# Attention and feed-forward on one core: eight more attention slots early in the main loop, a scale traced one job later, and eight subtractions moved to GpSimd

## The chip, the core and the metric

The kernel runs on one core of a Trainium2 chip. The metric is the device time of one execution in microseconds (us). Five engines work in parallel, each on its own queue and in order: TensorE (PE), VectorE (DVE), ScalarE (ACT), GpSimd (POOL) and SyncE (SP), which here only issues DMAs.

## The reference

Causal attention with a decay bias feeds a two-matrix feed-forward:

```python
batch, n_heads, seq, head_dim = (8, 8, 576, 64)
scores = scale * np.matmul(q, k.transpose(0, 1, 3, 2))
cum = np.cumsum(np.maximum(s, 0.0), axis=-1)
bias = -(cum[:, :, :, None] - cum[:, :, None, :])
scores = np.where(causal, -1000000000.0, scores + np.minimum(bias, 0.0))
attn = np.exp(scores - np.max(scores, axis=-1, keepdims=True))
attn = attn / (np.sum(attn, axis=-1, keepdims=True) + 1e-09)
out = np.matmul(attn, v)
...
x = out.transpose(0, 2, 1, 3).reshape(4608, 512)
h = x @ w_in                     # 512 x 2048
g = np.where(h >= 1, h, np.where(h <= -1, 0.0, (h + 1) ** 2 / 4))
y = g @ w_out                    # 2048 x 512
```

## The kernel before, in words

**Precision.** The weights arrive as 64-bit floats and are decoded on the chip into float32 (`Weights.decode`), scaled by a bound on their size (`Weights.scale`) and split into two float16 halves, high and low (`Weights.split`). Activations are split likewise. Each feed-forward product is three float16 matmuls: high by high, low by high, high by low.

**Attention** is cut into 64 jobs: 8 batches, two halves of the sequence (`hf` 0: 320 queries, `hf` 1: 256), four pairs of heads. A job is eight *slots*, `att_slot(j, k)`: k = 0 prepares Q and K; k = 1 and 5 handle V in half 0; k = 2 to 7 are six units of scores (`s` tiles, named `s<pair>_<tile>_<head>_<column>`, numbered by pair over all batches, 0 to 31). Each unit is two matmuls (L384, L385), a minimum on DVE (L390) and an exponential on ACT (L401); `weights_t` then makes float16 halves on POOL, ACT and DVE and transposes them with a DMA from SP into `pt`. At k = 7 the *previous* job's product with V is traced (`att_out`: the tile `px<pair>_<half>`, 18 or 30 matmuls), which fills a quarter of `x` for that batch and half. The score tiles and `px` share two PSUM buffers.

**Feed-forward** is 256 steps, one for each batch, half and tile of 128 hidden columns. A step is 12 matmuls `h<batch>_<half>_<tile>` (L501), an activation on ACT and DVE (L513, L516, L517), a split on ACT and POOL (L527, L528), and two steps later 12 matmuls into `y` (L540). The last three of the 12 matmuls of an `h` read the quarter of `x` that the last `px` of that batch and half fills.

**Order.** First, four jobs of attention run beside the decoding of the first weight; its scale (`row_wi`) and split follow. Then the main loop takes 512 values of `j`: each traces one or two attention slots and half a feed-forward step. In the first 32 values a generator feeds in the second weight (`w2_tasks`: eight chunks decoded, scale, eight chunks split, twice). A scheduler then orders each engine's instructions by priority and readiness; some are given a lead (`tc.high_priority`), so the order on an engine isn't the traced one.

**What the change touches.** `batch_v(b)` reduces V to a bound; `batch_scales_v(b)` carries it across partitions with two small matmuls on PE (`row_m`, `col_m`) and gives `ex`, which the copy of `px` into `x` needs. The loop over slots:

```python
for _ in range(1 if j >= 2 * NFT else 1 + (j % 4 == 3)):
    att_slot(t // 8, t % 8)
    t += 1
```

`NFT` is 16, so 40 slots are traced in the first 32 values of `j` and one for each value after. The split of the second weight: ACT writes the high half of chunk `c` (L221); for chunks in `POOL_LO` ACT also scales the weight in place (L226) and POOL subtracts (L227), for the others DVE does both in one instruction (L229). The output of chunk `c` lies where chunk `c - 2` was held, so the high half of a chunk waits for the low half two chunks earlier.

Of the kernel before, what the change touches and what calls it, by code (L numbers as in the profile page):

```python
# [25 lines left out]
NFT = DFF // P  # L26
# [27 lines left out]
Y_LAG = 2  # L54

ACT_LOW = {'wi': range(0, 16, 2), 'wo': range(0, 16, 2)}
POOL_LO = {'wi': (2, 3, 7, 11, 15), 'wo': range(1, 16, 2)}
POOL_SCALE = ('wi',)

K_POOL = range(12)  # L60
# [13 lines left out]
def attention_ffn(ctx: ExitStack, tc: tile.TileContext, qT, kT, vT, s, w_in, w_out, yT):  # L74
# [29 lines left out]
    def column_max(src, name):  # L104

        row = ps_s.tile([P, 512], F32, tag="s", name=f"row_{name}")
        T.transpose(row[:1, :P], src, ident)
        top = ap.tile([P, 1], F32, tag="top", name=f"top_{name}")
        V.tensor_reduce(top[:1], row[:1, :P], axis=AX, op=ALU.max)
        return top[:1]  # L110

    def spread(dst, top, name):

        t16 = ap.tile([P, 1], BF16, tag="t16", name=f"t16_{name}")
        V.tensor_copy(t16[:1], top)
        col = ps_s.tile([P, 512], F32, tag="s", name=f"col_{name}")
        T.matmul(col[:, :1], ones[:1], t16[:1], start=True, stop=True)
        V.tensor_copy(dst, col[:, :1])
# [45 lines left out]
    class Weights:  # L164
        def __init__(self, name, src, held, out, tags, groups):
# [5 lines left out]
            self.raw = {}  # L171
            self.act_low, self.pool_lo = ACT_LOW[name], POOL_LO[name]

# [76 lines left out]
    def batch_v(b):  # L250
        c = csc[b] = ap.tile([P, NPAIR], F32, tag="csc", name=f"c{b}")
        r = rcs[b] = ap.tile([P, NPAIR], F32, tag="rcs", name=f"rc{b}")
        for p in range(NPAIR):
            V.tensor_reduce(c[:, p:p + 1], vraw[b, p], axis=AX, op=ALU.max, apply_absolute_value=True)
        pow2floor(c, c, TINY)
        V.reciprocal(r, c)
        V.tensor_scalar(r, r, 4096.0, None, ALU.mult)

    def batch_scales_v(b):
        t = ap.tile([P, 1], F32, tag="mt", name=f"mt{b}")  # L260
        V.tensor_reduce(t, csc[b], axis=AX, op=ALU.max)
        m = msc[b] = ap.tile([P, 1], F32, tag="mb", name=f"mb{b}")
        spread(m, column_max(t, f"m{b}"), f"m{b}")
        r = ap.tile([P, 1], F32, tag="mr", name=f"mr{b}")
        V.reciprocal(r, m)
        e = exs[b] = ap.tile([P, NPAIR], F32, tag="ex", name=f"ex{b}")
        V.tensor_scalar(e, csc[b], r, 2.0 ** -12, ALU.mult, ALU.mult)
# [51 lines left out]
    def att_prep(n, hf):  # L319

        rq, rk = raws.pop((n, hf))
        q0, N, _ = HALF[hf]
        W = q0 + N
        cd = cumd[2 * n:2 * n + 2].rearrange("h l n -> l h n")
        A.activation(Q1[:, :, :N], rq, AF.Copy, scale=-0.125)
        if jobs.index((n, hf)) < CH_N:
            for hd in range(2):
                r = ch[2 * n + hd:2 * n + hd + 1]
                CUMQ.dma_start(Q2[D:D + 2, hd, :N].bitcast(F32), r[:, :, q0:W].bitcast(F32))
                CUMQ.dma_start(K2[D + 2:D + 4, hd, :W].bitcast(F32), r[:, :, :W].bitcast(F32))  # L330
        else:
            CUMQ.dma_start(Q2[D:D + 2, :, :N].bitcast(F32), cd[:, :, q0:W])
            CUMQ.dma_start(K2[D + 2:D + 4, :, :W].bitcast(F32), cd[:, :, :W])
        A.copy(K1[:, :, :W], rk)
        A.activation(Q2[:D, :, :N], rq[:D], AF.Copy, scale=-0.125)
        V.scalar_tensor_tensor(  # L336
            Q1[D:, :, :N], rq[D:], -0.125, Q1[D:, :, :N].bitcast(F32), ALU.mult, ALU.subtract
        )
        (G if jobs.index((n, hf)) in K_POOL else V).tensor_tensor(  # L339
            K2[:D, :, :W], rk[:D], K1[:D, :, :W].bitcast(F32), ALU.subtract  # L340
        )

    def v_prep(n):

        b, p = n // NPAIR, n % NPAIR
        v = vraw.pop((b, p))
        r = rcs[b][:, p:p + 1]
        VB = ap.tile([P, 2, SP], F16, tag="vb", bufs=1, name=f"vb{n}")
        G.memset(VB[:, :, S:], 0.0)
        G.tensor_scalar(VB[:, 0, :S], v, r, 1.0, ALU.mult, ALU.mult)  # L350
        if n < V_POOL:
            G.tensor_scalar(v, v, r, 1.0, ALU.mult, ALU.mult)
            G.tensor_tensor(VB[:, 1, :S], v, VB[:, 0, :S], ALU.subtract)
        vbs[n] = VB, v, r
# [105 lines left out]

    def batch_start(b):
        batch_v(b)
        batch_scales_v(b)

    jobs = [(NPAIR * b + p, hf) for b in range(B) for hf in range(2) for p in range(NPAIR)]

    def att_slot(j, k):

        if j < len(jobs):
            n, hf = jobs[j]  # L470
            if k == 0:
                att_prep(n, hf)
            if k == 1 and hf == 0:
                v_prep(n)
            if k == V_K and hf == 0:
                v_turn(n)
            if k >= 2:
                scores(n, *UNITS[hf][k - 2])
            if k == 3 and j + 1 < len(jobs):
                att_load(*jobs[j + 1])  # L480
            if k == 1 and j % (2 * NPAIR) == V_J and j // (2 * NPAIR) + 1 < B:
                load_v(j // (2 * NPAIR) + 1)
            if k == 5 and j + 1 < len(jobs) and jobs[j + 1][0] % NPAIR == 0 and jobs[j + 1][1] == 0:
                with tc.issue_after(ttr[0]):
                    batch_start(jobs[j + 1][0] // NPAIR)
        if k == OUT_K and 1 <= j <= len(jobs) and j != NPAIR:
            while j == len(jobs) and late:
                late.pop(0)()
            att_out(*jobs[j - 1])
# [80 lines left out]
    att_load(0, 0)  # L570
    load_v(0)
    batch_start(0)
    for j in range(NPAIR):
        for k in range(8):
            if k % 2 == 0:
                c = 4 * j + k // 2
                w1.decode(c)
                w1.load(c + 3)
            att_slot(j, k)
    while late:  # L580
        late.pop(0)()
    w1.scale(0, LEAST_A)
# [22 lines left out]
    for j in range(16 * NP):  # L605
        if j % 64 == 48 and j // 64 + 1 < B:
            batch_scales(j // 64 + 1)
            batch_y(j // 64 + 1)
        for _ in range(1 if j >= 2 * NFT else 1 + (j % 4 == 3)):
            att_slot(t // 8, t % 8)  # L610
            t += 1
        with tc.high_priority(offset=W2_LEAD):
            for _ in range(W2_RATE):
                next(tasks, None)
        if j >= 2 * NFT:
            ffn_step(j // 2, j % 2)
        elif j < NFT:
            ffn_step(j, 0)
        else:
            if j == NFT:  # L620
                with tc.high_priority(offset=FFN_LEAD):
                    g_split()
            m = 2 * (j // 8 % 2)
            for i in range(j % 8 * 2, j % 8 * 2 + 2):
                ffn_y(*ffn_q[i], ms=(m, m + 1))
            if j == 2 * NFT - 1:
                del ffn_q[:NFT]
# [32 lines left out]
```

## Time and profile before

| what | value |
|---|---|
| median of three runs | 1171.36 us (1170.36 to 1180.07) |
| the profiled execution | 1178.29 us, of which the span of its instructions is 1176.2 us |
| PE busy | 1009.5 us (86% of the span) |
| DVE busy | 892.6 us (76%) |
| ACT busy | 746.0 us (63%) |
| POOL busy | 691.0 us (59%) |
| mean granted TensorE clock | 0.967 |

Busy time is a mean over stages; the stages differ, so the prediction reads the kernel in stretches of time. In rows of stretches, each engine's busy time stands beside the length, "PEclk" is the clock granted to TensorE as a share of full speed, and the DMA share is that of 16 engines. In rows of the timeline, the number in brackets is how long the engine had been idle, and what released it.

### The profile page before, as it was taken

What the parts mean: (1) busy time and instruction counts of PE and PEld (TensorE: products, weight loads), DVE (VectorE), ACT (ScalarE), POOL (GpSimd) and SP (SyncE); (2) the same over time, 40 slices, a digit from 0 to 9 for tenths busy, and PEclk for the clock granted to TensorE, in tenths of its full rate; (3) what the DMA queues carried; (4) which work ended last, traced back from release to release, by engine and by line L of the source; (5) the groups of instructions that cost most, each with busy time, mean ns of one, the idle gap of its engine ahead of it and who ended that gap; (6) DMA issues with size and microseconds to landing.
All of it is one profiled execution on the core that took longest, in us unless ns stands there. A gap on an engine that the chain in (4) does not pass through costs nothing.

```text
span 1176.2 us, 25135 instructions
## 1 busy us (share of the span) xinstructions
PE 1009.5 (86%) x8470; PEld 776.6 (66%) x8470; DVE 892.6 (76%) x2404; ACT 746.0 (63%) x1719; POOL 691.0 (59%) x1169
## 2 busy tenths in 40 slices
PE   0234678699999999799998999899989999899998
PEld 0122345487767867587767867677768867686787
DVE  6879998778777877768777777778778877787633
ACT  4656677567656765767557665667557764777533
POOL 3876268676556664656546654656557564675522
PEclk9997999799998999999999999899999999899999
DMA  8885536867637773776638672876547753767310
GB/s 243 206 195 138 165 85 145 159 139 153 130 73 180 147 148 74 166 139 144 131 84 168 152 149 65 173 142 156 119 98 172 153 133 75 163 132 157 74 34 19
DMA packets 343081, 158.04 MB, mean 134 GB/s; under 512 B 291112, under 2 KB 324264, under 8 KB 342952
## 3 DMA queue, kind: packets, MB, share of 16 engines
q1 hardware_dynamic: 333248, 146.50, 59.0%
q10 hardware_dynamic: 9704, 9.93, 2.7%
q8 instruction: 67, 1.10, 0.4%
q14 instruction: 62, 0.51, 0.1%
HBM read 75.33 MB, written 9.73 MB: 72 GB/s over the span
## 4 chain that ended last, share of the span: by engine, by line
PE 42%; DVE 8%; DMA 5%; POOL 5%; issue 3%; ACT 1%; DVEq 0%; ACTq 0%; POOLq 0%
PE y L540 18%; PE h L501 17%; DMA pt<-pb 4%; PE px L447 3%; POOL pb L422 2%; DVE pb L428 2%; PE s L384 2%; PE s L385 2%; DMA vt<-vb 2%; POOL pb L425 1%; DVE p L390 1%; DVE K L339 1%; DVE h L516 1%; DVE Q L336 1%; POOL vb L350 1%
## 5 line engine op out<-in xcount | busy, mean ns | idle before, releaser
L501 PE MATMUL h<-x,WI 128*128 128x256 f16 (+1 forms) x3072 | 453.0, 292 | 23.4 <-DVE u L517 21.0
L540 PE MATMUL y<-g,WO 128*128 128x256 f16 (+1 forms) x3072 | 453.2, 291 | 17.3 <-POOL g L528 7.4
L501 PEld LDWEIGHTS <-WI 128*128 128x128 f16 x3072 | 292.3, 100 | 118.2 <-issue 28.2
L540 PEld LDWEIGHTS <-WO 128*128 128x128 f16 x3072 | 287.1, 99 | 108.7 <-issue 19.3
L528 POOL TENSOR_TENSOR g<-u,g 128x320 f16<-128x320 f32 (+1 forms) x256 | 199.2, 778 | 209.1 <-ACT g L527 203.9
L513 ACT ACTIVATE u<-h,ub,us 128x320 f32<-128x320 f32 (+1 forms) x256 | 149.3, 584 | 171.8 <-PE h L501 146.7
L401 ACT ACTIVATE p<-p,mn 64x64 f32<-64x64 f32 (+4 forms) x320 | 178.8, 559 | 113.6 <-DVE mn L390 96.4
L516 DVE SCALAR_TENSOR_TENSOR h<-h,ws,u 128x320 f32<-128x320 f32 (+1 forms) x256 | 133.0, 520 | 118.4 <-ACT u L513 117.9
L422 POOL TENSOR_SCALAR pb<-p,rs 64x128 f16<-64x128 f32 (+4 forms) x160 | 113.7, 711 | 152.2 <-DVE rs L418 118.6
L384 PE MATMUL s<-K,Q 128*128 128x288 f32 (+4 forms) x384 | 150.9, 395 | 43.8 <-DVE mn L390 33.3
L428 DVE SCALAR_TENSOR_TENSOR pb<-p,rs,pb 64x128 f16<-64x128 f32 (+4 forms) x160 | 135.8, 849 | 52.0 <-POOL pb L422 51.6
L425 POOL TENSOR_TENSOR pb<-p,pb 64x128 f16<-64x128 f32 (+4 forms) x160 | 165.0, 1032 | 9.2
L390 DVE CUSTOM_DVE_ANT_0 p<-s,mask 64x64 f32<-64x64 f32 (+4 forms) x320 | 134.8, 422 | 41.1 <-PE s L385 36.7
L517 DVE SCALAR_TENSOR_TENSOR u<-u,r,h 128x320 f32<-128x320 f32 (+1 forms) x256 | 130.2, 510 | 7.5
L423 ACT ACTIVATE p<-p,rs 64x64 f32<-64x64 f32 (+4 forms) x160 | 89.3, 559 | 67.2 <-DVE rs L418 60.6
L385 PE MATMUL s<-K,Q 68*128 68x288 f32 (+4 forms) x384 | 121.8, 319 | 9.8 <-ACT p L423 5.5
L447 PE MATMUL px<-pt,vt 128*64 128x256 f16 (+3 forms) x1536 | 87.7, 260 | 38.0 <-DMA pt<-pb 21.8
L384 PEld LDWEIGHTS s<-K,Q 128*128 128x128 f32 (+1 forms) x384 | 74.3, 194 | 68.2 <-DVE mn L390 42.4
L527 ACT CAST g<-u 128x320 f16<-128x320 f32 (+1 forms) x256 | 108.1, 422 | 10.6 <-DVE u L517 10.6
L447 PEld LDWEIGHTS <-vt 128*64 128x64 f16 x1536 | 73.2, 113 | 61.5 <-issue 40.3
L424 POOL TENSOR_SCALAR pb<-p 64x128 f16<-64x128 f32 (+4 forms) x160 | 90.9, 569 | 6.0 <-ACT p L423 2.9
L385 PEld LDWEIGHTS s<-K,Q 68*128 68x128 f32 (+1 forms) x384 | 75.8, 198 | 12.2 <-ACT p L423 5.9
(116 smaller groups left out, 961.4 us busy)
## 6 DMA issues: line engine op xcount, KB each, us to landing
rk<-in_k_dram SPq DMA_DIRECT2D x64, 288.0 KB
rq<-in_q_dram SPq DMA_DIRECT2D x64, 160.0 KB
rk<-in_k_dram SPq DMA_DIRECT2D x64, 160.0 KB
v<-in_v_dram SPq DMA_DIRECT2D x32, 288.0 KB
wir<-in_moe_w_in_dram SPq DMA_DIRECT2D x16, 512.0 KB
rq<-in_q_dram SPq DMA_DIRECT2D x64, 128.0 KB
wor<-in_moe_w_out_dram SPq DMA_DIRECT2D x16, 512.0 KB
out_dram<-o ACTq DMA_DIRECT2D x32, 160.0 KB
```

Source lines behind the costliest of these rows:

```text
L384: T.matmul(sc[:R, :c1 - c0], Q1[:, hd, qo:qo + R], K1[:, hd, c0:c1], start=True, stop=False)
L385: T.matmul(sc[:R, :c1 - c0], Q2[:KC, hd, qo:qo + R], K2[:KC, hd, c0:c1], start=False, stop=True)
L390: ttr[0] = V.tensor_tensor_reduce(out=Pt[:R, c0:c1], in0=sc[:R, :c1 - c0], in1=mask[:R, mo:mo + c1 - c0], scale=1.0, scalar=3.0e38 if mn i ...
L401: A.activation(Pt[:R, :W], Pt[:R, :W], AF.Exp, bias=m2[:R], scale=-1.0, accum_out=sums[n, i][:R, hd:hd + 1])
L425: G.tensor_tensor(los[1], pw, his[1], ALU.subtract)
L428: V.scalar_tensor_tensor(los[0], pv, rs[:R, :1], his[0], ALU.mult, ALU.subtract)
L447: T.matmul(px[hd * D:(hd + 1) * D, lo:N], VT[:, vl * NB + j, hd * D:(hd + 1) * D], PT[:, 4 * j + 2 * hd + pl, lo:], start=(m == 0), stop=( ...
L501: T.matmul(h[:, :N], WI[4 * kt + ft // 4][:, wl, ft % 4 * P:(ft % 4 + 1) * P], x[:, kt, xl], start=(n == 0), stop=(n == 3 * NKT - 1),)
L513: first = A.activation(u, h[:, :N], AF.Relu, bias=ubi[b], scale=usc[b]).ins
L516: V.scalar_tensor_tensor(h[:, :N], h[:, :N], wsc[b], u, ALU.mult, ALU.max)
L528: G.tensor_tensor(g[:, 1], u, g[:, 0], ALU.subtract)
L540: T.matmul(ys[b, hf, m][:, :N], WO[8 * (m // 2) + ft // 2][:, wl, c0:c0 + P], g[:, gl], start=(ft == 0 and n == 0), stop=(ft == NFT - 1 an ...
```

## The change

It does three things. Between j = 32 and j = 95, eight values of `j` (35, 43, ... 91) trace two attention slots instead of one, so from there on attention is traced eight slots further ahead of the feed-forward, and its last slot comes at j = 471 instead of 479. For batch 0, `batch_scales_v` is traced after slot 6 of job 0 instead of ahead of all jobs. And all sixteen chunks of the second weight are in `POOL_LO`, so the eight even chunks are scaled on ACT and subtracted on POOL instead of on DVE.

```diff
-POOL_LO = {'wi': (2, 3, 7, 11, 15), 'wo': range(1, 16, 2)}
+POOL_LO = {'wi': (2, 3, 7, 11, 15), 'wo': range(16)}
...
     def batch_start(b):
         batch_v(b)
-        batch_scales_v(b)
+        if b:
+            batch_scales_v(b)
...
             att_slot(j, k)
+            if j == 0 and k == 6:
+                batch_scales_v(0)
...
-        for _ in range(1 if j >= 2 * NFT else 1 + (j % 4 == 3)):
+
+        for _ in range(1 + (j % 4 == 3 if j < 2 * NFT else j % 8 == 3 and j < 6 * NFT)):
             att_slot(t // 8, t % 8)
```

The scheduler turns this into another order on every engine. Three places follow; names carry the buffer's number at the end. Lines after the change are one or two further down (L501 becomes L502, L540 becomes L541).

PE at its very start, before (`row_m0` and `col_m0` are the two small matmuls of the V scale, `s0_...` the scores of job 0):

```order
L107 MATMUL row_m0_183<-ident_77,mt0_180 1x128
L117 LDWEIGHTS ones_82
L117 MATMUL col_m0_189<-t16_m0_187,ones_82 128x1
L384 MATMUL s0_0_0_0_227<-K1_90,Q1_89 64x64
L385 MATMUL s0_0_0_0_227<-K2_92,Q2_91 64x64
```

And the same place with the change:

```order
L384 MATMUL s0_0_0_0_211<-K1_90,Q1_89 64x64
L384 MATMUL s0_0_1_0_219<-K1_90,Q1_89 64x64
...
L385 MATMUL s0_2_0_0_286<-K2_92,Q2_91 128x320
L107 MATMUL row_m0_297<-ident_77,mt0_294 1x128
L117 LDWEIGHTS ones_82
L117 MATMUL col_m0_303<-t16_m0_301,ones_82 128x1
L384 MATMUL s0_2_1_0_312<-K1_90,Q1_89 128x320
```

The V scale stood ahead of all scores; now five of the six units of job 0 stand ahead of it.

PE where batch 2 passes into batch 3, before (`px11_1` is the last product with V of batch 2; `h2_1_...` the feed-forward that reads it; `s12` and `s13` are scores of batch 3):

```order
L385 MATMUL s12_1_1_0_6050<-K2_92,Q2_91 128x192
L540 MATMUL y2_0_0_5308<-g2_0_12_5928,WO7_131 128x320
...
L385 MATMUL s12_2_0_0_6079<-K2_92,Q2_91 128x320
L385 MATMUL s12_2_1_0_6108<-K2_92,Q2_91 128x320
L447 MATMUL px11_1_6122<-pt11_1_5723,vt11_4816 64x256
...
L385 MATMUL s13_0_0_0_6212<-K2_92,Q2_91 64x64
L501 MATMUL h2_1_0_6174<-x2_1_5395,WI12_120 128x256
```

With the change:

```order
L385 MATMUL s12_1_1_0_5933<-K2_92,Q2_91 128x192
L541 MATMUL y2_0_0_5428<-g2_0_12_6070,WO6_130 128x320
...
L502 MATMUL h2_0_15_6229<-x2_0_4260,WI11_119 128x320
...
L385 MATMUL s12_2_1_0_5991<-K2_92,Q2_91 128x320
L502 MATMUL h2_1_0_6305<-x2_1_5262,WI4_112 128x256
...
L541 MATMUL y2_0_0_5428<-g2_0_12_6070,WO7_131 128x320
...
L447 MATMUL px11_1_6005<-pt11_1_5606,vt11_4676 64x256
L502 MATMUL h2_1_1_6351<-x2_1_5262,WI0_108 128x256
```

Between `px10_1` and `px11_1` PE had 57 feed-forward matmuls and now has 92; between `px11_1` and `px12_0` it had 51 and now has 55. The 39 come out of the stretches from `px12_0` to `px14_1`, and it is so at each of the six passages from batch 1 on. Counted in steps of 24 matmuls, a `px` stands half a step to two steps further ahead of the feed-forward than before, and the last one, `px31_1`, three steps. At the first products of batch 1, `px4_0`, 432 feed-forward matmuls stand ahead instead of 444.

POOL in the second group of the second weight's split, before (`WO` tiles; `pb` tiles are the halves of the attention weights):

```order
L422 TENSOR_SCALAR pb2_3_1570<-p2_3_0_1551,rs2_3_1571 128x4x128
L227 TENSOR_TENSOR WO9_133<-WO11_135,WO9_133 128x512
L381 MEMSET p3_3_0_1750 128x64
L424 TENSOR_SCALAR pb2_3_1570<-p2_3_1_1561 128x4x128
L425 TENSOR_TENSOR pb2_3_1570<-p2_3_1_1561,pb2_3_1570 128x4x128
```

With the change:

```order
L424 TENSOR_SCALAR pb2_4_1685<-p2_4_1_1660 128x5x128
L227 TENSOR_TENSOR WO8_132<-WO10_134,WO8_132 128x512
L227 TENSOR_TENSOR WO9_133<-WO11_135,WO9_133 128x512
L425 TENSOR_TENSOR pb2_4_1685<-p2_4_1_1660,pb2_4_1685 128x5x128
L381 MEMSET p3_4_0_1816 128x64
```

Chunk 8 has joined chunk 9 on POOL, and the pair stands a tile of attention weights later than chunk 9 stood.

## The prediction

> **What bounds the kernel now.** I read the page's busy times first, then busy times stretch by stretch, cut where a product with V (`px`) starts on PE, and then PE's waits.
>
> ```profile
> PE 1009.5 (86%) x8470; PEld 776.6 (66%) x8470; DVE 892.6 (76%) x2404; ACT 746.0 (63%) x1719; POOL 691.0 (59%) x1169
> ```
>
> The mean hides two kernels. The start, up to about 235 us:
>
> ```profile
> core 0: us, PE busy (x) PEld busy (x) DVE busy (x) ACT busy (x) POOL busy (x), PEclk, DMA share, GB/s
> 0.00:25.00 25.00, 0.37 (x1) 0.18 (x2) 16.05 (x35) 9.75 (x12) 7.36 (x19) 1.00 0.88 242
> 25.00:87.00 62.00, 20.51 (x104) 14.49 (x103) 51.72 (x149) 39.21 (x92) 46.69 (x73) 1.00 0.85 203
> 150.00:175.00 25.00, 18.94 (x116) 12.12 (x117) 24.84 (x46) 19.75 (x38) 16.27 (x16) 0.93 0.34 83
> 175.00:207.00 32.00, 27.62 (x216) 18.65 (x214) 27.55 (x60) 21.77 (x42) 27.26 (x31) 0.95 0.66 137
> 207.00:235.00 28.00, 17.47 (x130) 13.46 (x127) 21.33 (x81) 17.32 (x46) 17.96 (x34) 0.70 0.83 163
> ```
>
> Here PE mostly waits. DVE is the fullest engine (24.84 of 25 us at 150), POOL nearly as full from 175 on, the DMA engines above 80% in the first 87 us. After that PE is the bound: from the first `px` of batch 2 to its last but one,
>
> ```profile
> 366.70:469.30 102.60, 100.29 (x868) 78.02 (x866) 77.73 (x214) 65.24 (x155) 59.24 (x103) 1.00 0.61 127
> ```
>
> PE is busy for 100.29 of 102.60 us at full clock. It falls short at one place in each batch, from the last but one `px` of a batch to the first of the next. All six passages, and the one at 469 in its two parts (before and after the batch's last `px`):
>
> ```profile
> 339.30:366.70 27.40, 22.45 (x193) 17.44 (x192) 21.57 (x65) 19.60 (x52) 18.56 (x39) 0.88 0.75 166
> 469.30:494.60 25.30, 21.11 (x193) 16.84 (x192) 20.08 (x62) 17.55 (x47) 16.87 (x34) 0.93 0.76 158
> 602.20:627.70 25.50, 21.21 (x195) 16.80 (x196) 18.79 (x60) 18.57 (x50) 15.96 (x31) 0.93 0.86 143
> 732.30:759.20 26.90, 22.68 (x195) 17.55 (x194) 19.95 (x64) 18.25 (x49) 18.54 (x39) 0.87 0.77 170
> 863.80:889.20 25.40, 21.09 (x190) 16.44 (x189) 19.88 (x62) 17.57 (x47) 16.60 (x33) 0.93 0.76 160
> 991.50:1018.50 27.00, 22.82 (x195) 17.66 (x196) 21.57 (x65) 19.42 (x51) 18.35 (x36) 0.87 0.71 147
> ...
> 469.30:481.50 12.20, 10.43 (x100) 8.20 (x99) 9.78 (x33) 8.31 (x22) 7.59 (x13) 1.00 0.52 116
> 481.50:494.60 13.10, 10.69 (x93) 8.65 (x93) 10.30 (x30) 9.24 (x26) 9.28 (x22) 0.87 0.99 196
> ```
>
> Length less PE busy: 4.95, 4.19, 4.29, 4.22, 4.31 and 4.18 us idle, 26.1 in all. One less the clock, times the length, is time lost to a slower clock: 3.3, 1.8, 1.8, 3.5, 1.8 and 3.5, 15.7 in all. A smaller loss is at the seven places where half 0 passes into half 1:
>
> ```profile
> 279.70:291.60 11.90, 10.71 (x91) 8.18 (x90) 9.09 (x26) 8.30 (x20) 5.58 (x9) 1.00 0.82 178
> ...
> 1060.60:1072.80 12.20, 10.88 (x92) 8.20 (x92) 9.84 (x26) 8.88 (x21) 6.02 (x9) 1.00 0.81 178
> sum 87.40, PE 76.42 PEld 57.26 DVE 70.95 ACT 64.20 POOL 43.49; mean PE 10.92 PEld 8.18 DVE 10.14 ACT 9.17 POOL 6.21
> ```
>
> That is 87.40 - 76.42 = 11.0 us over seven. What PE waits for from 345 us on:
>
> ```profile
> PE px L447 <- DMA pt<-pb: 16.3, 12, 2.1
> PE s L384 <- DVE mn L390: 11.3, 12, 2.1
> PE y L540 <- POOL g L528: 7.1, 5, 2.6
> ```
>
> So: the transposed attention weights for a `px`, and scores that find no PSUM buffer until DVE has read one. At a passage PE has no feed-forward left to fill these gaps, since the next half's `h` needs the very `px` that it waits for.
>
> **The V scale, moved behind five units of job 0.**
>
> ```profile
> 14.74 1.54 POOL L339 TENSOR_TENSOR K<-rk,K 64x640 fp32r<-64x640 f32 x1 [9.72 <-ACT K L334]
> ...
> 23.05 0.37 PE L107 MATMUL row_m<-ident,mt 128*1 128x128 f32 x1 [23.05 <-DVE mt L261]
> 26.16 0.32 PE L384 MATMUL s<-K,Q 128*64 128x64 f32 x1
> ...
> 72.59 0.16 DVE L208 TENSOR_REDUCE t_wi<-peak_wi 128x1 f32<-128x16 f32 x1
> ...
> 85.26 1.65 PE L447 MATMUL px<-pt,vt 128*64 128x320 f16 x18 [5.14 <-DVE rs L418]
> 86.84 0.37 PE L107 MATMUL row_wi<-ident,t_wi 128*1 128x128 f32 x1
> ```
>
> K is ready at 14.74 + 1.54 = 16.28, yet the first score starts at 26.16, behind `row_m` and `col_m`: up to 9.9 us to win. It counts, because the first weight's scale (`row_wi`, 86.84) stands on PE behind a `px` of attention and not behind the decoding, which was done at 72.59. But DVE has only 25 - 16.05 = 9 us free in the first 25 and is 83% busy until 87, with the decoding on the same queue, and the weight loads keep the DMA engines at 85%. Ends 0 and 9.9; I take the middle, **5 us gained**. SP's queue speaks for caution too: the loads of the last two weight chunks, which stood ahead of job 1's last two transposes, now stand behind them, so a late transpose holds a load. What is late next is job 1's Q and K, then the decoding.
>
> **Eight chunks from DVE to ACT and POOL.**
>
> ```profile
> L229 DVE SCALAR_TENSOR_TENSOR WO<-WO,r_wo,WO 128x512 f16<-128x512 f32 x8 | 8.4, 1047 | 0.0
> L226 ACT ACTIVATE WO<-WO,r_wo 128x512 f32<-128x512 f32 x8 | 5.7, 711 | 0.0
> L227 POOL TENSOR_TENSOR WO<-WO,WO 128x512 f16<-128x512 f32 x8 | 10.6, 1323 | 0.0
> ```
>
> DVE loses 8 x 1.047 = 8.4 us, ACT gains 8 x 0.711 = 5.7, POOL 8 x 1.323 = 10.6, all between 150 and 207. Four of the eight fall where DVE is full (4.2 us) and POOL has 8.7 us free; the other four fall where POOL has 32 - 27.26 = 4.7 us free for 5.3. Behind a late chunk wait its successor two chunks on, the `pb` tiles queued on POOL, and `y` with everything behind it on PE. Ends: 8.4 gained, 10.6 lost. I take half of the 4.2 us of the full stretch, **2 us gained**.
>
> [...] The rows above give 1.323 to 1.047, or 1.26 times. [...]
>
> **Eight slots more.** No work is added: the same slots are traced, earlier. On PE the order shows what it does. One feed-forward matmul takes
>
> ```profile
> 455.72 1.63 PE h L501 x12
> ...
> 1142.15 1.31 PE y L540 x12
> ```
>
> 0.136 us at 320 columns, 0.109 at 256; 0.122 between. Five passages get 35 more ahead of the batch's last `px` and 4 more behind it, 39 x 0.122 = 4.8 us of work, taken from stretches where PE is full and which get shorter by as much. The first passage gets 24 more and 9 fewer, 1.8 us.
>
> What a passage gives back lies between two ends. If only its first part fills, 12.20 - 10.43 = 1.8 us, since the second keeps its 2.4 us of idle (DMA is at 0.99 there). If the attention chain sets the length of the whole passage, all 4.2 us idle fill. The chain gets some start, as 13 matmuls now stand between the last score of job 12 and `px11_1`, where there were none; so the middle, 3.0: 5 x 3.0 + 1.8 = **16.8 us gained**. At the seven half-to-half places about 31 more matmuls arrive, 31 x 0.122 = 3.8 us, against 11.0 / 7 = 1.6 us idle; ends 0 and 11.0, middle **5.5 us gained**. At `px4_0` 12 fewer feed-forward matmuls are done, so 12 x 0.122 = **1.5 us** move from the waiting start to the full part. At the end, 495 instead of 444 matmuls follow the last `px`; there PE is full,
>
> ```profile
> 1125.00:1150.00 25.00, 25.00 (x230) 21.55 (x226) 8.98 (x19) 9.14 (x22) 6.27 (x9) 1.00 0.08 27
> ```
>
> so they cost there what they save earlier. The moved slots issue no more DMAs than before, each still in its slot's turn on SP.
>
> **Sum**: -5 - 2 - 16.8 - 5.5 + 1.5 = -27.8 us. The profiled execution took 1178.3 us (its span 1176.2 and 2.1 around it), 6.9 above the median of 1171.4; a like execution would take 1150.5, and against the median I forecast **1143.6 us**.
>
> **Rivals.**
>
> *The clock stays up too.* I left the 15.7 us of slower clock at the passages in place. If PE, with 13 more matmuls close behind the last `px`, is no longer throttled, they go as well: 1143.6 - 15.7 = **1128 us**. For it: the clock is 1.00 in every first part and below 1 only where PE thins out. Against: the second part gains just 4 matmuls. [...]
>
> *The change does not do what it says.* The lead is eight slots in the code but half a step to two steps on PE, because the scheduler runs attention as fast as it thinks it can go. If the passages stay as long and the full stretches do not shorten (real waits there replace the matmuls taken out), only the start gains: 1171.4 - 5 - 2 + 1.5 = **1166 us**. For it: in the stretches that give matmuls up, attention needs DVE and ACT in the same order as before. Against: PE is busy 100.29 of 102.60 us there.
>
> *Slower: the last `px` of each batch comes later.* The 35 matmuls ahead of it take 4.3 us and the gap they fill is 1.8 us, so it starts 2.5 us later, in five passages 12.5 us. If attention (DMA at 0.99 behind it) sets the pace from there on, that is lost: 1166 + 12.5 = **1178 us**, and up to 1189 if POOL's 10.6 us also land on the path. It decides if PE's idle time between the passages grows by more than what the passages win. Against it speaks the same full PE; for it, PE waits 16.3 us for transposes already.
>
> **Chances and range.** Forecast 0.58 (1132 to 1156), clock up 0.12, no lead 0.18, slower 0.12. The predicted time is that of the first. The range takes in the clock's case and the case without a lead: 1125 to 1172. One per cent of 1171 is 12 us, about what a measurement of this kernel can tell from no change. Faster by more: 0.58 and 0.12, less a little of the first, 0.68. Slower by more (above 1183) half of the last, 0.06. The rest, 0.26, within 1%.
>
> **What would show it.** First score at 17 us, `row_wi` near 82; no DVE L229 on `WO`, sixteen L227 on POOL, `y` of batch 0 not waiting longer for POOL than before; in the first part of a passage PE busy without a gap; passages still dropping to 0.87 or not; and 51 x 0.109 = 5.6 us more feed-forward between the last `px` and the end. I am wrong if POOL's chunks hold PE between 175 and 235, if the passages stay as they are, or if the stretches between them get idle time.

## The result and the profile after

The changed kernel takes 1129.61 us (median of four runs, 1128.06 to 1130.64), beside 1170.92 us for the kernel before (median of four, 1170.36 to 1180.07): a ratio of 0.9628, with a 95% interval of 0.958 to 0.9677. That is 41.3 us faster, where the prediction said 27.8. The profiled execution took 1128.06 us, with a span of 1126.2 us and a mean granted clock of 0.975 (before 0.967). As the profiled execution of before lay 7.4 us above its median and this one 1.6 below, the two profiles differ by 50.0 us in span, not by 41.3.

The page's busy times after the change:

```profile
PE 988.1 (88%) x8470; PEld 771.8 (69%) x8470; DVE 876.6 (78%) x2396; ACT 745.2 (66%) x1727; POOL 693.1 (62%) x1177
```

PE runs the same 8470 matmuls and is busy 21.4 us less. Where the span shrank is seen when it is cut at the first `px` of batch 1 (`px4_0`) and at the last but one `px` of all (`px30_1`). Stretches of the kernel before, and then of the changed kernel (length, then busy time and instructions of each engine, the clock, the DMA share, GB/s):

```profile
0.00:235.10 235.10, 119.70 (x752) 80.01 (x752) 198.84 (x512) 150.62 (x296) 143.46 (x203) 0.91 0.69 167
235.10:1110.30 875.20, 827.79 (x7157) 644.52 (x7156) 670.16 (x1846) 572.85 (x1373) 529.19 (x942) 0.98 0.64 133
1110.30:1176.20 65.90, 61.98 (x567) 52.08 (x566) 23.61 (x48) 22.50 (x52) 18.37 (x25) 1.00 0.11 30
```

```profile
0.00:233.30 233.30, 120.48 (x750) 82.06 (x750) 195.94 (x505) 155.60 (x305) 151.23 (x210) 0.89 0.69 167
233.30:1052.60 819.30, 799.15 (x7108) 632.85 (x7107) 654.48 (x1841) 564.99 (x1369) 521.38 (x940) 1.00 0.67 143
1052.60:1126.20 73.60, 68.46 (x616) 56.92 (x615) 26.18 (x51) 24.60 (x55) 20.50 (x27) 0.98 0.10 27
```

The start is 1.8 us shorter, the middle 55.9, the end 7.7 longer, as 49 more matmuls stand there. So nearly all of it is the middle, and there the clock column says 1.00 instead of 0.98. The start, by parts:

```profile
0.00:25.00 25.00, 3.29 (x11) 2.18 (x12) 17.17 (x46) 11.86 (x20) 6.75 (x19) 1.00 0.89 251
25.00:87.00 62.00, 17.74 (x94) 13.04 (x94) 56.59 (x143) 37.38 (x85) 47.80 (x78) 1.00 0.89 202
...
150.00:175.00 25.00, 18.35 (x122) 12.08 (x122) 23.60 (x51) 19.84 (x40) 22.11 (x22) 0.86 0.42 95
175.00:207.00 32.00, 28.13 (x184) 18.91 (x183) 21.63 (x53) 22.93 (x42) 28.39 (x34) 0.84 0.60 123
```

In the first 25 us PE now has 11 matmuls instead of one: the scores no longer stand behind the V scale, and the first of them starts at 14.49 us instead of 26.16. DVE is busy 56.59 of the next 62 us (before 51.72). Between 150 and 207 DVE is eased (21.63 of 32, before 27.55) and POOL loaded (22.11 of 25, before 16.27). The clock there is lower than before, 0.86 and 0.84 instead of 0.93 and 0.95.

The middle. First the full stretch of batch 2 and then the six passages from the last but one `px` of a batch to the first of the next:

```profile
356.40:451.90 95.50, 93.95 (x828) 74.52 (x827) 75.64 (x212) 64.22 (x154) 60.46 (x106) 1.00 0.67 143
```

```profile
331.00:356.40 25.40, 23.60 (x208) 18.14 (x207) 20.73 (x66) 18.85 (x50) 16.40 (x35) 0.93 0.75 154
451.90:477.00 25.10, 24.78 (x234) 19.68 (x233) 21.03 (x67) 19.37 (x52) 16.27 (x32) 1.00 0.75 151
575.50:600.50 25.00, 24.72 (x232) 19.66 (x231) 20.97 (x67) 19.30 (x52) 16.33 (x32) 1.00 0.70 153
698.10:723.30 25.20, 24.75 (x234) 19.66 (x233) 20.98 (x67) 19.36 (x52) 16.81 (x34) 1.00 0.72 160
818.40:843.40 25.00, 24.72 (x232) 19.64 (x231) 20.68 (x67) 19.36 (x52) 16.97 (x32) 1.00 0.74 152
941.20:967.00 25.80, 24.74 (x234) 19.65 (x233) 20.90 (x67) 19.34 (x52) 17.04 (x35) 1.00 0.62 135
sum 151.50, PE 147.31 PEld 116.44 DVE 125.29 ACT 115.57 POOL 99.82; mean PE 24.55 PEld 19.41 DVE 20.88 ACT 19.26 POOL 16.64
```

A passage is still about 25 us long, but five of the six now hold some 39 matmuls more, PE is idle for 151.50 - 147.31 = 4.2 us in all six (before 26.1), and the clock is 1.00 in five and 0.93 in the first. The two parts of the second passage, and the seven half-to-half places (their sum):

```profile
451.90:467.00 15.10, 15.10 (x137) 11.58 (x137) 12.40 (x38) 11.01 (x28) 10.18 (x18) 1.00 0.54 117
467.00:477.00 10.00, 9.68 (x100) 8.10 (x99) 8.63 (x30) 8.36 (x25) 6.09 (x14) 1.00 1.05 201
```

```profile
sum 96.20, PE 96.14 PEld 76.98 DVE 80.26 ACT 68.59 POOL 63.68; mean PE 13.73 PEld 11.00 DVE 11.47 ACT 9.80 POOL 9.10
```

The first part has no gap, and at the half-to-half places 0.06 us of 11.0 is left. PE's waits in the part from the first passage to the last `px`:

```profile
PE s L384 <- DVE Q L336: 5.4, 6, 1.3
PE y L541 <- POOL g L529: 5.3, 7, 0.8
PE px L447 <- DMA pt<-pb: 3.3, 3, 1.6
PE s L384 <- DVE mn L390: 2.0, 4, 0.8
```

The two waits that led the list before, for transposed weights (16.3 us) and for a free score buffer (11.3), are down to 3.3 and 2.0.

One measure is used throughout below: the five batches from `px8_0` to `px28_0`. That is the same feed-forward work in every kernel, whatever the lead is. Before, and after:

```profile
366.70:1018.50 651.80, 613.34 (x5294) 476.96 (x5294) 499.26 (x1386) 424.45 (x1021) 389.17 (x698) 0.98 0.65 134
```

```profile
356.40:967.00 610.60, 594.25 (x5293) 470.57 (x5292) 487.79 (x1385) 420.35 (x1021) 386.97 (x700) 1.00 0.68 143
```

From 130.4 us a batch to 122.1.

### The profile page after: what moved, and what is told of

It reads as the page before. It is cut to its first block, busy times and chain, and to the rows that moved or that the text cites. A ratio compares the mean times of both kernels' runs of the same rounds, so it can differ in the third digit from the quotient of the medians.

```text
span 1126.2 us, 25201 instructions
## 1 busy us (share of the span) xinstructions
PE 988.1 (88%) x8470; PEld 771.8 (69%) x8470; DVE 876.6 (78%) x2396; ACT 745.2 (66%) x1727; POOL 693.1 (62%) x1177
## 4 chain that ended last, share of the span: by engine, by line
PE 48%; DVE 6%; POOL 5%; issue 3%; ACT 3%; DMA 2%; ACTq 0%; DVEq 0%; POOLq 0%
PE h L502 20%; PE y L541 20%; PE px L447 3%; PE s L384 3%; PE s L385 2%; DMA pt<-pb 2%; DVE pb L428 1%; DVE Q L336 1%; POOL g L529 1%; POOL pb L422 1%; ACT u L514 1%; ACT p L401 1%; POOL vb L350 1%; POOL pb L425 1%; DVE p L390 1%
## 5 line engine op out<-in xcount | busy, mean ns | idle before, releaser
L502 PE MATMUL h<-x,WI 128*128 128x256 f16 (+1 forms) x3072 | 464.7, 291 | 30.3 <-DVE u L518 24.7
L541 PE MATMUL y<-g,WO 128*128 128x256 f16 (+1 forms) x3072 | 456.7, 288 | 7.5 <-POOL g L529 5.3
L502 PEld LDWEIGHTS <-WI 128*128 128x128 f16 x3072 | 291.2, 99 | 124.0 <-issue 34.2
L541 PEld LDWEIGHTS <-WO 128*128 128x128 f16 x3072 | 287.3, 98 | 91.8 <-issue 12.5
L529 POOL TENSOR_TENSOR g<-u,g 128x320 f16<-128x320 f32 (+1 forms) x256 | 204.0, 797 | 162.1 <-ACT g L528 161.3
L422 POOL TENSOR_SCALAR pb<-p,rs 64x128 f16<-64x128 f32 (+4 forms) x160 | 97.3, 608 | 165.2 <-DVE rs L418 105.1
L384 PE MATMUL s<-K,Q 128*128 128x288 f32 (+4 forms) x384 | 149.2, 391 | 55.9 <-DVE mn L390 25.9
L425 POOL TENSOR_TENSOR pb<-p,pb 64x128 f16<-64x128 f32 (+4 forms) x160 | 172.8, 1080 | 9.2
L428 DVE SCALAR_TENSOR_TENSOR pb<-p,rs,pb 64x128 f16<-64x128 f32 (+4 forms) x160 | 143.1, 894 | 43.0 <-POOL pb L422 42.7
L447 PE MATMUL px<-pt,vt 128*64 128x256 f16 (+3 forms) x1536 | 82.4, 258 | 18.3 <-DMA pt<-pb 8.1
```

Source lines behind the costliest of these rows:

```text
L384: T.matmul(sc[:R, :c1 - c0], Q1[:, hd, qo:qo + R], K1[:, hd, c0:c1], start=True, stop=False)
L425: G.tensor_tensor(los[1], pw, his[1], ALU.subtract)
L428: V.scalar_tensor_tensor(los[0], pv, rs[:R, :1], his[0], ALU.mult, ALU.subtract)
L447: T.matmul(px[hd * D:(hd + 1) * D, lo:N], VT[:, vl * NB + j, hd * D:(hd + 1) * D], PT[:, 4 * j + 2 * hd + pl, lo:], start=(m == 0), stop=( ...
L502: T.matmul(h[:, :N], WI[4 * kt + ft // 4][:, wl, ft % 4 * P:(ft % 4 + 1) * P], x[:, kt, xl], start=(n == 0), stop=(n == 3 * NKT - 1),)
L529: G.tensor_tensor(g[:, 1], u, g[:, 0], ALU.subtract)
```

## The experiments

Three theories stood at the start, called A, B and C below. *Lead*: the eight slots alone give the gain, by work that fills PE's gaps and keeps its clock. *Start*: the two small edits give their 5 and 2 us. *Lucky order*: a scheduler that is disturbed anywhere could have hit upon a better order. Each kernel below is the kernel before with the lines shown, and ran beside the kernel before on the same chip.

**Each part alone.** The eight slots:

```diff
-        for _ in range(1 if j >= 2 * NFT else 1 + (j % 4 == 3)):
+        for _ in range(1 + (j % 4 == 3 if j < 2 * NFT else j % 8 == 3 and j < 6 * NFT)):
```

> The eight slots alone, without the moved V scale and with the second weight's split as before. Theory A (the lead makes the whole gain): the order on PE gives the passages the same 92 and 55 feed-forward matmuls as in the full change, so 1129 to 1134 us, a ratio of 0.964 to 0.968, passages of about 25 us with the clock at 1.00. Theory B (the edits of the start count as forecast, 5 and 2 us): 1135 to 1138 us. Theory C (a lucky order; nothing hangs on the lead): anywhere between 1130 and 1171.

Measured: 1132.43 us beside 1172.71, a ratio of 0.9638 (0.9597 to 0.9678). The slots alone give nearly all of it. Their five batches take 613.8 us, and the passages look like those of the whole change.

The V scale, traced after slot 6 of job 0:

```diff
-        batch_scales_v(b)
+        if b:
+            batch_scales_v(b)
...
+            if j == 0 and k == 6:
+                batch_scales_v(0)
```

> The moved V scale alone. Its passages have the 57 and 48 to 51 matmuls of the kernel before. A: 1168 to 1172 us, since the first feed-forward matmul came only 2.5 us earlier in the full change and the first product of batch 1 only 1.8; passages drop to 0.77 to 0.93 of the clock as before. B: 1166 us.

Measured: 1174.94 us, a ratio of 1.0 (0.9973 to 1.0028): nothing. Why is on the timeline around the first weight's scale, of this kernel:

```profile
83.13 0.37 PE L107 MATMUL row_wi<-ident,t_wi 128*1 128x128 f32 x1
...
84.37 3.04 DVE L428 SCALAR_TENSOR_TENSOR pb<-p,rs,pb 128x384 f16<-128x384 f32 x1 [0.79 <-POOL pb L422]
87.33 0.27 DVE L109 TENSOR_REDUCE top_wi<-row_wi 1x1 f32<-1x128 f32 x1
...
88.88 0.16 PE L117 MATMUL col_wi<-t_wi,ones 1*128 1x1 bf16 x1 [5.38 <-DVE t_wi L115]
```

`row_wi` runs at 83.13, 3.7 us earlier than in the profile of before. But its result is read by DVE, and there a product with attention weights stands ahead that takes 3.04 us, so `col_wi` comes at 88.88 instead of 90.02. In the kernel before the same product stands a little later in the chain and takes 1.29 us:

```profile
88.09 1.29 DVE L428 SCALAR_TENSOR_TENSOR pb<-p,rs,pb 128x384 f16<-128x384 f32 x1
...
90.02 0.16 PE L117 MATMUL col_wi<-t_wi,ones 1*128 1x1 bf16 x1 [2.81 <-DVE t_wi L115]
```

What differs in the rows is the work beside it. With the later V scale, POOL's sum for K runs at the same time (`84.39 2.60 POOL L339`, a row of the same timeline); in the kernel before that sum was over when the product began (81.92 + 2.61 = 84.53 us, before 88.09). In the whole change the product takes 3.03 us, beside the same sum. No run moved the sum alone. Of 3.7 us 1.1 are left, and in this execution the first `px` of batch 1 starts at 236.9 us, not earlier than the 235.1 of before. The time is 2.9 us above what theory A expected, where the kernel before itself took 1172.71; the interval reaches to 3.2 us gained, which leaves out the 5 us of the forecast for this edit alone.

The second weight's chunks:

```diff
-POOL_LO = {'wi': (2, 3, 7, 11, 15), 'wo': range(1, 16, 2)}
+POOL_LO = {'wi': (2, 3, 7, 11, 15), 'wo': range(16)}
```

> All low halves of the second weight on ACT and POOL, alone. A: 1168 to 1174 us, the DVE time saved being made up for by POOL. B: 1169 us. If POOL's 10.6 us land on the path, up to 1182 us.

Measured: 1174.7 us, a ratio of 0.9998 (0.9974 to 1.0021): nothing either. Its stretch from 175 to 207 us:

```profile
175.00:207.00 32.00, 26.78 (x215) 17.99 (x213) 24.33 (x53) 24.04 (x45) 31.45 (x35) 1.00 0.68 142
```

DVE is eased from 27.55 to 24.33 us, but POOL goes from 27.26 to 31.45 of 32: one full engine takes the other's place. Between 150 and 240 us, PE's waits of `y` for POOL's chunks (L227) grow from 3.1 to 4.7 us. The interval, from 3.0 us gained to 2.5 lost, does not exclude the 2 us of the forecast.

**The slots later.** The same eight slots, traced between j = 256 and 319, in batch 4:

```diff
+        for _ in range(1 + (j % 4 == 3 if j < 2 * NFT else j % 8 == 3 and 16 * NFT <= j < 20 * NFT)):
```

> The eight slots alone, but traced in the feed-forward of batch 4 (j = 256 to 319) instead of batches 0 and 1. The order on PE leaves the passages up to batch 3 into 4 as before (57 and 51 matmuls) and gives those from 5 into 6 and 6 into 7 the 92 and 55, the one from 4 into 5 part of it. A: the gain goes by the number of passages behind the slots, about 0.44 of it: 1150 to 1157 us, first passages at 0.87 of the clock or less, last two at 1.00. C: no such split, near 1130 or near 1171.

Measured: 1157.42 us, a ratio of 0.9844 (0.9803 to 0.9884). The five batches one by one:

```profile
363.80:491.20 127.40, 120.44 (x1059) 94.05 (x1058) 98.44 (x275) 84.40 (x204) 77.79 (x141) 1.00 0.67 134
491.20:625.40 134.20, 126.31 (x1059) 97.44 (x1058) 100.11 (x281) 86.94 (x208) 77.67 (x140) 0.95 0.67 136
625.40:751.30 125.90, 121.35 (x1050) 95.09 (x1049) 99.49 (x277) 84.13 (x204) 78.82 (x143) 0.97 0.64 139
751.30:872.60 121.30, 118.50 (x1061) 94.12 (x1060) 95.51 (x276) 83.37 (x202) 74.81 (x136) 1.00 0.67 142
872.60:997.80 125.20, 119.53 (x1061) 94.15 (x1062) 97.88 (x278) 84.03 (x206) 77.92 (x142) 1.00 0.66 138
```

The first two batches, ahead of the slots, take 127.4 and 134.2 us, much as before (127.9 to 133.1); the last two, behind them, 121.3 and 125.2, as with the whole change (120.1 to 123.6). The gain begins where the lead begins, which a lucky order would not explain. The time is 0.4 us above the range of theory A. The clock did not follow it everywhere: the second passage, still without the lead, ran at 1.00.

**How much lead.** Sixteen slots instead of eight:

```diff
+        for _ in range(1 + (j % 4 == 3 if j < 2 * NFT else j % 4 == 3 and j < 6 * NFT)):
```

> Sixteen extra slots between j = 32 and j = 95 instead of eight, and nothing else of the change. The order has the same 92 and 55 feed-forward matmuls at the passages and the same 495 after the last px as with eight. Lead theory: same time as the eight slots alone, 1129 to 1136, since PE has no gap left to fill there. If every slot of lead is worth something: 1095 to 1120. If attention ahead of its time crowds the start: 1140 to 1175.

Measured: 1135.84 us beside 1176.74, a ratio of 0.9651 (0.9603 to 0.9699), no different from eight. And one slot only:

```diff
+        for _ in range(1 + (j % 4 == 3 if j < 2 * NFT else j == 35)):
```

> The kernel before with one extra slot (at j = 35) instead of eight. In the order it puts 72 feed-forward matmuls between the last but one and the last px of a batch (before 57, with eight slots 92) and 51 from there to the next px (before 51), and none more after the last px of all (444). Lead theory: the gaps of PE's first part of a passage fill (1.8 us x 6 = 11), those at the half-to-half places fill at least in part (0 to 11), the second part keeps its 2.4 us and the slower clock stays in part; 1145 to 1160. Theory of a lucky order (any change of the order could have won): no relation to the number of slots, 1130 or 1172. If the gain is one for each of the eight slots: 41/8, 5 us, 1167.

Measured: 1157.14 us, a ratio of 0.9831 (0.9787 to 0.9874): one slot already gives 19.6 us, nearly half. Its passages, then its five batches and its seven full stretches (sum):

```profile
335.10:359.50 24.40, 21.59 (x209) 17.34 (x209) 18.20 (x64) 18.00 (x50) 15.36 (x30) 1.00 0.78 160
...
sum 143.00, PE 129.38 PEld 103.78 DVE 109.50 ACT 105.77 POOL 93.97; mean PE 21.56 PEld 17.30 DVE 18.25 ACT 17.63 POOL 15.66
```

```profile
359.50:996.10 636.60, 605.33 (x5287) 470.48 (x5286) 493.59 (x1386) 421.69 (x1021) 395.44 (x701) 1.00 0.67 138
```

```profile
sum 708.80, PE 685.69 PEld 532.40 DVE 553.28 ACT 461.72 POOL 440.42; mean PE 97.96 PEld 76.06 DVE 79.04 ACT 65.96 POOL 62.92
```

This kernel is the most telling one. The clock is 1.00 in all six passages, where a part of the slower clock was expected to stay: five of the six second parts still have their 51 feed-forward matmuls, and they are idle for 1.7 us on average. The passages have 13.6 us idle instead of 26.1, the half-to-half places 1.3 instead of 11.0. If these gains added up, it would be 12.5 + 9.7 + 15.7 (the clock) = 37.9 us; measured were 19.6. Of the difference, 11.5 us came back in the full stretches: idle there (708.80 - 685.69, less the 1.3 at the half-to-half places) is 21.8 us, where before, counted alike, it was 10.3. The other 6.8 are not accounted for. The longest sums of its waits:

```profile
PE y L540 <- POOL g L528: 7.4, 11, 1.0
...
PE h L501 <- DVE u L517: 4.9, 11, 1.1
```

No wait is long; there are many short ones, and new among them `h` behind the activation on DVE. With eight slots the same idle outside the half-to-half places is 15.9 us, which is also more than before: part of the gain is given back there too, but a smaller part.

**Is the slower clock a cost by itself?** Two kernels add useless work to PE at the passages of the kernel before, where it had time. In the first the added matmuls stand behind the batch's last `px`:

```diff
-        T.matmul(sc[:R, :c1 - c0], Q1[:, hd, qo:qo + R], K1[:, hd, c0:c1], start=True, stop=False)
+        twice = 2 if i < 3 and n >= 4 and n % NPAIR == 1 else 0
+        for z in range(twice + 1):
+            T.matmul(sc[:R, :c1 - c0], Q1[:, hd, qo:qo + R], K1[:, hd, c0:c1], start=True, stop=z < twice)
```

> The kernel before, with the first score matmul of each unit run three times (two more, which only repeat it) in the second job of each batch's half 0, from batch 0's second half on: the job whose scores stand at a passage. That is some 12 to 18 more matmuls of 0.03 to 0.14 us at a passage, work that helps nothing. If the slower clock at a passage comes from PE being thinly busy there, the clock rises from 0.87 to 0.93 toward 1.00 and most of the added work is paid by it and by the gaps: 1165 to 1175. If the clock has another cause (load of the other engines or of the DMAs at the passage), it stays at 0.87 to 0.93 and the added work is paid in part: 1174 to 1186.

Measured: 1174.16 us beside 1176.74, a ratio of 0.9987 (0.9962 to 1.0012). Two of its second parts, and its five batches:

```profile
344.80:356.80 12.00, 10.72 (x107) 8.98 (x107) 9.68 (x29) 8.88 (x26) 9.12 (x20) 1.00 0.96 200
476.70:489.10 12.40, 12.03 (x107) 10.22 (x109) 9.27 (x29) 8.90 (x26) 8.75 (x22) 0.86 0.99 201
```

```profile
356.80:1015.10 658.30, 619.28 (x5351) 484.36 (x5350) 497.00 (x1387) 425.27 (x1022) 394.80 (x704) 0.98 0.64 134
```

With 12 more matmuls the second parts are shorter in this trace: 74.7 us for all six instead of 84.0 (though 76.8 also with the later V scale alone, which adds no work there). Two of them run at full clock and four at 0.86 to 0.88 (before 0.77 to 0.87), and the mean granted clock of its ten executions is 0.971, beside 0.964 of the kernel before. So with PE busier there the clock was higher. But the time of the kernel is the same, within both of the expected ranges, and a batch takes 131.7 us: what the passages won, the full stretches lost (728.7 us instead of 717.7). The added matmuls also take PE time themselves, some 6 us in six passages by the busy time that they add in the next kernel (62.4 us in first parts before, 68.8 there, so 0.09 us for each of 72), so the clock was not tried alone. The same matmuls for the job ahead of it, so that they stand in the first part:

```diff
+        twice = 2 if i < 3 and n >= 4 and n % NPAIR == 0 else 0
```

> The kernel before, with the first score matmul of each unit run three times in the first job of each batch's half 0 from batch 1 on (12 more matmuls a batch, which only repeat work): its scores stand in the first part of a passage, where PE had 1.8 us of gaps and a full clock. If the slower clock in the second part follows from gaps in the first, it rises from 0.77 to 0.87 toward 1.00 there. If the second part's own thin work sets it, it stays at 0.77 to 0.87. On the time: if the slower clock is a cost that adds up by itself (15.7 us in the passages), a clock back at 1.00 gives 1156 to 1162; if the time won there returns as waits in the stretch behind, because attention sets the pace of a batch, 1168 to 1178 whatever the clock does.

Measured: 1174.56 us beside 1175.65, a ratio of 0.9991 (0.9976 to 1.0007). The two parts of one passage, and the five batches:

```profile
464.30:476.50 12.20, 11.46 (x112) 9.47 (x112) 9.22 (x33) 7.74 (x20) 6.34 (x12) 1.00 0.52 116
476.50:491.30 14.80, 12.10 (x92) 9.08 (x92) 11.64 (x30) 11.06 (x31) 10.51 (x20) 0.77 0.88 206
```

```profile
361.90:1013.30 651.40, 620.84 (x5348) 484.29 (x5347) 500.22 (x1385) 426.01 (x1025) 390.08 (x695) 0.97 0.62 134
```

The first part's idle falls from 1.8 us to 0.7 and the second part's clock stays at 0.77. So the gap in the first part isn't what slows the clock of the second; over all executions, too, the clock is 0.965 beside 0.963. The busy share of the whole second part doesn't settle it either, since with one slot 9.54 of 11.7 us went at 1.00. The traces show more when they are cut finely. In the kernel before, from 240 us on to 15 us before the end, the granted clock falls seven times, each time from 1.00 to 0.50, for 3.41 or 6.83 us. Here is the stretch ahead of a fall and the fall itself there, and then a stretch at the same passage with one slot:

```profile
483.07:486.49 3.42, 1.47 (x12) 1.10 (x12) 2.40 (x5) 2.82 (x8) 2.59 (x7) 1.00 0.98 204
486.49:489.90 3.41, 2.99 (x12) 2.14 (x12) 3.41 (x13) 1.97 (x8) 3.10 (x5) 0.50 0.89 188
```

```profile
478.22:481.64 3.42, 2.42 (x19) 1.84 (x17) 3.23 (x12) 2.52 (x10) 3.34 (x6) 1.00 0.97 215
```

Ahead of each of the seven, PE was busy for 0.86 to 1.99 us of 3.41, and in the changed kernel for 1.95 of 3.41 ahead of its one fall in that time (at 348.94 us). A thin stretch was not followed by a fall every time: at 776.63 us of the kernel before PE was busy for 1.47 of 3.42 us, and the clock stayed at 1.00. In the kernel before a second part at 0.87 holds a fall of 3.41 us, one at 0.77 a fall of 6.83. So in these two traces each fall stands right behind one thin stretch, and the busy share of the whole passage doesn't tell where. And 60 repeated matmuls in five batches cost nothing (651.4 us, before 651.8): at these places PE has time to give away as long as the useful work is missing.

**What the small edits are worth on top of the slots.** The slots with the V scale, which ran beside the sixteen slots:

> The eight slots and the later V scale, without the eight chunks on ScalarE and GpSimd. If the second weight's chunks are worth nothing on top of the slots either: 1128 to 1132, as the whole change. If the V scale is worth nothing on top of the slots: 1131 to 1135, as the slots alone. If the chunks cost what GpSimd is slower by: 1118 to 1126.

Measured: 1136.45 us, a ratio of 0.9657 (0.9603 to 0.9711). Then three kernels on one chip: the whole change, the slots with the chunks, the slots alone.

> The whole change once more, beside the slots alone on the same chip. If the V scale and the second weight's chunks are worth nothing also on top of the slots: within 1.5 us of the slots alone. If they are worth what they were forecast at (5 and 2) once the slots have removed the waits behind them: 5 to 7 us below the slots alone. If only some: 2 to 4 below.

> The eight slots and all chunks of the second weight on ScalarE and GpSimd, with the V scale where it was. If the chunks are worth something on top of the slots: 2 to 4 us below the slots alone, and as the whole change. If not: as the slots alone within 1.5 us, and any lead of the whole change is then the V scale's or that of both together.

> The eight slots alone once more, as the measure for the two kernels beside it: 1129 to 1137.

Measured, beside 1175.65 us of before: the whole change 1129.65 us, ratio 0.96 (0.9581 to 0.962); slots with the chunks 1134.87, 0.9644 (0.9626 to 0.9663); slots alone 1131.4, 0.9617 (0.9596 to 0.9637). The whole change and the slots alone differ by 1.8 us with intervals that overlap (by their ends, from 6.6 us faster to 2.8 slower), so whether the two small edits together are worth anything isn't settled. Neither of them alone helps on top of the slots: with the V scale the time missed all three expected ranges, and with the chunks it is 3.5 us above the slots alone, where no change or 2 to 4 us less was expected. But the whole change is 5.2 us below the slots with the chunks, and these two intervals do not meet. So on top of both, the later V scale does gain about what it was forecast at; why only there, no run shows. No version beat the whole change.

## Why the prediction was right, and where it was not

The direction, the place (the passages and half-to-half places) and the cause (feed-forward work brought to where PE waited) were right. The sum came to 27.8 us instead of 41.3 because the terms for the half-to-half places and the clock, and perhaps that for the passages, were too small, and the two for the small edits too large. The waits that grew in the full stretches (from 10.3 to 15.9 us) had no term. The measured 1129.61 us lies below the 1132 to 1156 given to the forecast, and beside the 1128 of the rival whose clock stays up. The mechanism of that rival came true; that its time fits so well is luck, since it keeps 7 us for the small edits and only 5.5 for the half-to-half places.

**The V scale (5 us) and the chunks (2 us)** gave nothing that alone could be measured, and together 1.8 us on top of the slots, which is not clear of noise. The first score came at 14.49 us, before the 17 looked for. The forecast that `row_wi` would come near 82 held; after the change it stands at 81.70:

```profile
81.70 0.37 PE L107 MATMUL row_wi<-ident,t_wi 128*1 128x128 f32 x1
82.95 3.03 DVE L428 SCALAR_TENSOR_TENSOR pb<-p,rs,pb 128x384 f16<-128x384 f32 x1 [0.79 <-POOL pb L422]
82.96 2.60 POOL L339 TENSOR_TENSOR K<-rk,K 64x1152 fp32r<-64x1152 f32 x1
...
87.46 0.16 PE L117 MATMUL col_wi<-t_wi,ones 1*128 1x1 bf16 x1 [5.38 <-DVE t_wi L115]
```

The step that failed is "It counts, because the first weight's scale (`row_wi`, 86.84) stands on PE behind a `px` of attention". The scale is a chain over PE, DVE and PE, and I had followed only its first instruction. The next one reads the row on DVE, and it now waits there behind the product that takes 3.03 us beside POOL's sum. Of 5.1 us at `row_wi`, 2.6 are left at `col_wi` and 1.8 at `px4_0`. Of the 2.6 lost on the way to `col_wi`, 1.7 are the longer product (3.03 instead of 1.29) and 0.8 is DVE's wait for POOL ahead of it. Of the chunks I had written that half of the full stretch's relief would arrive; with the chunks alone, POOL's new load there (31.45 of 32 us) is the likely reason that it didn't. That they cost no more on POOL than the forecast had was right: 16 at 1253 ns, less than the 1323 of before. The ratio of 1.26 (POOL's 1.323 us for a chunk to DVE's 1.047), though, compared unlike work, a subtraction with a scaling and subtraction in one; for one and the same sum (L339, 64x1152) the kernel before has 2710 ns on POOL and 1350 on DVE.

```profile
L227 POOL TENSOR_TENSOR WO<-WO,WO 128x512 f16<-128x512 f32 x16 | 19.9, 1253 | 1.7 <-ACT WO L226 1.7
```

**The six passages (16.8 us).** I put the five later ones between 1.8 us (only the first part fills) and 4.2 (the attention chain sets the whole passage) and took 3.0. By the two profiles the upper end was right: a passage is about as long as before, 25.0 to 25.8 us, and all but 4.2 of the 26.1 us idle are filled, which makes the term 21.9. But the profile of before was a long execution. The V scale alone and the chunks alone, whose passages hold as many matmuls as before, show 21.4 and 20.9 us idle, and by these the term is about 17, as forecast. That the attention chain sets the length of a passage isn't shown: with eight slots PE itself is busy for 24.7 of some 25 us, and with one slot a passage took 23.5 to 24.4.

**The half-to-half places (5.5 us)** were mis-sized by the choice of the middle: the end of 11.0 came, to within 0.06.

**The clock** was left in place and made a rival with an estimated chance of 0.12. By the same count (one less the clock, times the length) its loss at the passages went from 15.7 us to 1.8, so 13.9 us less. "The second part gains just 4 matmuls" was the argument against, and it looked at the wrong thing. The second part shrank from 13.1 to 10.0 us with 4 matmuls more, as its waits went away, and PE is busy for 9.68 of these 10.0 us. That leaves 0.32 us idle in all of it, where PE had been idle for 1.4 to 2.6 us of the 3.41 ahead of each fall in the kernel before. The waits there were short one by one: the longest of the kernel before from 345 us on was 2.6 us. What ties the clock to them, no run shows.

**The twelve matmuls (1.5 us)** are too few to be told apart in these stretches. Those behind the last `px` are there: the end is longer by what was forecast for them (5.6 us), and somewhat more (7.7, in which `px30_1` to `px31_1` is counted too).

Do the corrected terms give the whole? For the five batches, which went from 651.80 to 610.60 us: PE's idle time fell from 38.46 to 16.35, by 22.1 us, and the slower clock by 14.5 (its five passages 12.4; one full stretch before, 107.6 us at 0.98, 2.1). That is 36.6 of 41.2 us. As PE also waits while the clock is slow, 14.5 is an upper count. The other 4.6 us or more are less busy time at full clock for as many matmuls; why, no run shows. Within the 22.1 us, passages gave 18.8 and half-to-half places 8.4, and the rest of the full stretches lost 5.1.

**The slower rival** (attention sets the pace and the later last `px` is lost) had a true part. The first part of a passage did become longer, 15.1 us instead of 12.2, by 2.9 where the rival said 2.5. But the second part became shorter by as much or more. And the idle time between the passages did grow, which the prediction named as the sign, by 5.1 us in five batches against 18.8 won. With a lead of one slot it takes back 10.4. The rival by which nothing moves fell: the full stretch of batch 2 shrank from 102.6 us to 95.5.

**What the terms are not.** The two kernels with repeated work and the one with one slot speak against taking idle time and clock at a passage for costs that add up singly. Passages and full stretches (`px4_0` to `px30_1`) take 875.2 us before and 876.4 and 875.1 us with repeated work, though their passages alone are 157.5, 147.7 and 164.0. Where attention has no more lead, a faster passage seems only to make PE wait later. That attention's own chain then sets the pace of a batch fits these runs, but no run here sped up that chain itself, so it is inferred.

## What to carry to other kernels

When one engine is full for most of a loop and starves at the same place in each round, trace the producer some steps ahead: the work that fills the gap is there already, and here one slot gave nearly half of the gain, eight all of it, sixteen no more. Of a saved time on one engine, follow the result to the next queue that reads it before counting it, and look at what will run beside the work that stands ahead there. Size a gap from more than one execution, since here the idle time of the passages was 26.1 us in one profile and about 21 in two others with as many matmuls there. Terms read from one place of a profile add up only if the places behind it don't wait in turn.

## What the runs showed of the hardware

TensorE's granted clock fell at places where no wait was longer than 2.6 us and PE was still busy for about 80% of the time (10.69 of 13.1 us at 0.87). In the kernel before, from 240 us on to 15 us before the end, it was then 0.50 for 3.41 or 6.83 us, seven times, and PE was busy for 0.86 to 1.99 of the 3.41 us ahead of each (1.47 of 3.42 us in the row above). It stayed up with 12 useless matmuls there (10.72 of 12.0 us at 1.00, though 12.03 of 12.4 at 0.86 in another passage of the same execution) and with useful work ahead of it (9.68 of 10.0 us at 1.00), and not with useless work in the 12 us ahead of it (12.10 of 14.8 us at 0.77). It also stayed up behind 1.47 of 3.42 us at 776.63 us in the kernel before.

One and the same VectorE product (L428, 128x384, the one ahead of `col_wi`) took 3.03 us in the whole change and 3.04 with the V scale alone, where GpSimd's sum for K (L339, 2.60 us) ran beside it, and 1.29 in the kernel before, where it did not.
